# 64-row contraction tails of the w1, V, K and Q products run as row-tile pairs, and PSUM evacuated two banks at a time, in a fused attention and MLP block

## The chip, the cores and the metric

The kernel runs on one core of one Trainium2 chip. The metric is the device time of one execution in microseconds (us). Each execution also has a *span*, the time from its first to its last instruction; here the time is 1.7 to 2.9 us more than the span. Stage times below are read on the span's clock. Every run lists the clock granted to TensorE.

The engines are PE (TensorE; PEld is its weight load), ACT (ScalarE), DVE (VectorE), POOL (GpSimd) and SP (which here only issues DMAs).

## The reference

```
xn = layernorm(x)                       # x: 2048 x 448, bf16
# A: linear attention, 16 heads of 28
q, k, v = xn @ wqkv
phi(t)  = [softmax(t @ w_phi), softmax(-(t @ w_phi))]      # per head
A       = (phi(q) @ (phi(k)^T v)) / (phi(q) . sum phi(k) + 1e-6) @ wo
# B: MLP with token shifts
h   = gelu(layernorm(xn) @ w1)          # four column quarters, shifted by +1, -1, +2, -2 tokens
x1  = xn + shifted(h) @ w2
B   = x1 + gelu(layernorm(x1) @ w3) @ w4                   # w3: 448 x 1792
out = x + A + B
```

What matters for this change is the 448. It is contracted in every product with xn, and 448 = 3 x 128 + 64: three full passes of 128 rows through the PE array and a *tail* of 64 rows.

## The kernel before

One program covers three stages, which overlap at their edges:

1. **Head.** The layer norm of 16 token tiles (statistics on DVE; scales on POOL; the multiply-add `ln_apply` of even tiles on POOL and odd ones on DVE from tile 4 on). The normalized tiles are transposed into `xnT`: tiles 0 to 11 by PE, tiles 12 to 15 by DMA. V of tiles 0 to 7 and the w1 product follow. w_phi is folded into the q and k weights (`fold`).
2. **K/Q stage.** K, Q, the later V tiles, w2, and the accumulation `kv_tile`.
3. **Tail stage.** The w3 product, with w4, the numerators of the attention and the output woven in.

A recorder gathers all operations in program order, each goes to its engine's queue, and semaphores are worked out from the tiles that are read and written. So each engine runs its own operations strictly in the order of the program text. All matmuls are recorded by one helper line (L186 before, L188 after); one goes by tile names instead of lines.

```python
# loads: rows 64..127 of the fourth row block are zero (a memset), so that a tail is a full 128-row matmul
def load_rows(dst, src):
    R.dma(dst[:, 0:3, :], src[0:384, :].rearrange("(c p) d -> p c d", p=128))
    R.dma(dst[0:64, 3, :], src[384:448, :])
# ... (cut)
R.ew(dve, "memset", xn[:, :, D:512], 0.0)           # columns 448..511 of xn
R.ew(dve, "memset", wv[64:128, 3, :], 0.0)
R.ew(dve, "memset", w1[64:128, 3, :], 0.0)
# ... (cut)
def ln_apply(eng, dst, src, rst, i):
    R.ew(eng, "tensor_scalar", dst, src, rst[:, i, 1:2], rst[:, i, 0:1], op0=ALU.add, op1=ALU.mult)

def ln1_apply(a, n, engs):
    for i in range(a, a + n):
        ln_apply(engs[i % len(engs)], xn[:, i, 0:D], xtok[:, i, :], rs, i)

def w1_chunk(g, m):                                 # 4 slots: three full passes and the zero-padded tail
    b = bank(2, 3, 4)
    for kc in range(KC):
        R.mm(b[0:CR, :], w1[:, kc, CR*m:CR*m+CR], xnT[:, kc, 512*g:512*g+512], kc == 0, kc == KC - 1)
    R.act(hT[0:CR, m, 2+512*g:2+512*g+512], b[0:CR, :], ACT.Gelu_apprx_tanh)

def k_tile(i):                                      # v_tile and q_chunk have the same form
    b = rot_b()                                     # a ring of six banks in this stage
    for kc in range(KC):
        R.mm(b[:, 0:D], xnT[:, kc, 128*i:128*i+128], wpk[:, kc, :], kc == 0, kc == KC - 1)
    R.act(phik[:, i, 0, :], b[:, 0:D], ACT.Exp)
    R.act(phik[:, i, 1, :], b[:, 0:D], ACT.Exp, scale=-1.0)
    # ... (cut: sums on DVE, the softmax's multiply on POOL)

def w3_quad(q):                                     # already uses row-tile pairs
    gf = [divmod(4 * q + k, FC) for k in range(4)]
    for k, (g, fc) in enumerate(gf):
        for kc in range(3):
            R.mm(banks[k][:, :], w3[:, kc, 128*fc:128*fc+128], gT[:, g % 2, kc, :], kc == 0, False)
    for k, (g, fc) in enumerate(gf):
        lo = 64 * (k % 2)
        R.mm(banks[k][:, :], w3[lo:lo+64, 3, 128*fc:128*fc+128], gT[lo:lo+64, g % 2, 3, :], False, True)
    for k, (g, fc) in enumerate(gf):
        R.act(h3T[:, g % 2, fc, :], banks[k][:, :], ACT.Gelu_apprx_tanh)
# ... (cut)
for g in (2, 3):                                    # end of the head
    for m in range(NM):
        fold(3 - g, m)
        w1_chunk(g, m)
for i in range(NT):                                 # the K/Q stage: a fine weave of single banks
    k_tile(i)
    if i >= 2:
        kv_tile(i - 2)
    if i % 2 == 0:
        v_tile(8 + i // 2)
    else:
        w2_tile(i // 2)
    q_chunk(*divmod(i, 4))
    # ... (cut: ln_scale, g_apply, g_T)
```

`w3_quad` shows the idea that the change extends. It puts four outputs in four banks and does their full passes first. Then come the four 64-row tails, alternately on rows 0 to 63 and rows 64 to 127. The tail rows of both operands lie on both halves, so that two tails run at once.

The softmax here doesn't subtract the row's maximum and nothing guards it: scores larger than these inputs give would overflow.

## Time and profile before

| | before |
|---|---|
| time | 200.66 us, median of 3 runs (200.6 to 200.78) |
| span of the profiled run | 198.6 us |
| head (to the first K matmul) | 34.6 us |
| K/Q stage (to the first w3 quad) | 44.4 us |
| tail stage | 119.6 us |

The first view is the page of the kernel before: busy time of each engine with its share of the span, then the shares of the chain of work that ended last.

```profile
PE 185.4 (93%) x1103; PEld 98.3 (49%) x1113; DVE 109.4 (55%) x249; ACT 87.2 (44%) x167; POOL 102.9 (52%) x155
...
PE 67%; POOL 12%; DVE 11%; DMA 3%; ACT 2%; issue 2%; SPq 1%; DVEq 0%; POOLq 0%
```

PE is busy for 93% of the span and carries most of the chain. Only a PE slot removed, or a PE wait removed, can shorten the kernel.

The next view is PE's timeline of the kernel before, in pieces. Columns are: start in us, duration, engine, line, operation, output<-inputs, shapes, count and, in brackets, idle time before the group and what ended it. Groups overlap a little, since a matmul is pipelined into the next. So one takes the distance from start to start, the *cadence*, for what a group costs.

```profile
30.55 1.03 PE L186 MATMUL bank<-xnT,w 128*112 128x512 bf16 x4
...
34.61 0.92 PE L186 MATMUL bank<-wpk,xnT 128*128 128x448 bf16 x4
...
51.34 0.92 PE L186 MATMUL bank<-wpk,xnT 128*128 128x448 bf16 x4
52.10 0.55 PE L186 MATMUL bank<-phik,vaug 128*128 128x224 bf16 x4
...
53.24 1.03 PE L186 MATMUL bank<-xnT,wpq 128*112 128x512 bf16 x4
54.10 0.92 PE L186 MATMUL bank<-wpk,xnT 128*128 128x448 bf16 x4
...
83.34 3.29 PE L186 MATMUL bank<-gT,w 128*128 128x512 bf16 x16
86.57 0.56 PE L186 MATMUL bank<-phik,vaug 128*128 128x224 bf16 x4
```

Four 448-column slots take 52.10 - 51.34 = 0.76 us (0.19 each), four 512-column slots 54.10 - 53.24 = 0.86 us (0.2155 each), a kv tile 0.38 us. No brackets: from 41.04 us on, this stage runs without a gap. (Before that PE waits once, 0.76 us at 41.04, for a kv tile's input `phik` from POOL; not shown.) The Trainium skill, "TensorE: Matmul & The Clock Gate", Part 1, gives the warm start-to-start time as N / 2.4 GHz plus about 2.5 ns, 215.7 ns at 512 columns; this trace agrees.

The w3 quad has 12 full slots and 4 tails, which as pairs count for 2. That is 14 x 0.2155 = 3.02 us, but it takes 86.57 - 83.34 = 3.23. The weight loads of the kernel before show where the other 0.2 us lies:

```profile
86.02 0.11 PEld L186 LDWEIGHTS bank<-gT,w 64*128 64x128 bf16 x4 [0.42 <-issue]
86.56 0.31 PEld L186 LDWEIGHTS bank<-phik,vaug 128*128 128x128 bf16 x4 [0.42 <-issue]
```

Twice, weight loading pauses for 0.42 us: before the first 64-row load, and before the first full-row load after the tails. The next weights aren't loaded ahead across a change of mode. The Trainium skill, "TensorEngine Tiling (Array Packing)", Key Properties, says that changing the tiling mode drains TensorE; the trace agrees, and puts the price at about 0.1 us per change.

The last view of before is POOL's timeline in the head, where the layer norm is made. One period makes two tiles.

```profile
14.79 0.70 POOL L198 TENSOR_TENSOR rs<-rs,mhalf 128x2 f32<-128x2 f32 x1
15.59 0.82 POOL L198 TENSOR_SCALAR xn<-xtok,rs 128x448 bf16<-128x448 bf16 x1
...
17.05 0.70 POOL L198 TENSOR_TENSOR rs<-rs,mhalf 128x2 f32<-128x2 f32 x1
```

The period is 17.05 - 14.79 = 2.26 us, and no line has an idle time in brackets. POOL is the engine that limits when normalized tiles appear.

### The profile page before, as it was taken

To read this page: it belongs to the slowest core of one execution; us is meant where nothing else is said; L and a number is where in the kernel's file an instruction comes from. 1 tells how busy PE (TensorE), PEld (TensorE's weight loads), DVE (VectorE), ACT (ScalarE), POOL (GpSimd) and SP (SyncE) were. 2 spreads that over 40 slices of the span, in tenths; PEclk is the share of its full clock that TensorE was granted. 3 is DMA by queue.
4 is the path that set the end of the run, shared out by engine and by line. 5 is a ranking of instruction groups with operands and counts; after the bars stand their busy time and mean duration, and the time that the engine had idled before them with its cause. 6 is when DMAs were issued, how large, how long until landed. Compare 5 with 4: busy or idle time off the path is not lost.

```text
span 198.6 us, 2932 instructions
## 1 busy us (share of the span) xinstructions
PE 185.4 (93%) x1103; PEld 98.3 (49%) x1113; DVE 109.4 (55%) x249; ACT 87.2 (44%) x167; POOL 102.9 (52%) x155
## 2 busy tenths in 40 slices
PE   0699999989999999999989999999998999999984
PEld 0345566546566665454445454454454445545541
DVE  5497410388888888557853654534255355165531
ACT  2368899966677666844404304124120430440000
POOL 7568880075668996860439333144733330313370
PEclk9999999999999999999999999999999999999999
DMA  5994259950000121032023133010416202212211
GB/s 161 284 242 92 40 93 327 289 165 0 0 0 3 26 53 26 0 56 53 10 43 78 28 76 76 3 50 14 90 26 102 53 23 50 53 25 74 50 50 48
DMA packets 32619, 14.56 MB, mean 73 GB/s; under 512 B 24414, under 2 KB 32094, under 8 KB 32606
## 3 DMA queue, kind: packets, MB, share of 16 engines
q1 hardware_dynamic: 32606, 14.39, 30.3%
q8 instruction: 8, 0.13, 0.3%
q14 instruction: 5, 0.04, 0.1%
HBM read 6.91 MB, written 1.84 MB: 44 GB/s over the span
## 4 chain that ended last, share of the span: by engine, by line
PE 67%; POOL 12%; DVE 11%; DMA 3%; ACT 2%; issue 2%; SPq 1%; DVEq 0%; POOLq 0%
PE bank L186 66%; DVE vaug L198 8%; POOL vaug L198 4%; POOL xnT L198 3%; POOL g_tok L198 2%; DMA gT<-g_tok 2%; POOL rs L198 2%; PE bank L190 1%; DMA xnT<-xnT 1%; POOL phik L198 1%; DVE xn L198 1%; SPq L201 1%; ACT L194 1%; DVE st L198 1%; DVE ksum L198 1%
## 5 line engine op out<-in xcount | busy, mean ns | idle before, releaser
L194 ACT ACTIVATE phik<-bank 128x512 bf16<-128x512 f32 (+1 forms) x88 | 44.6, 585 | 68.1 <-PE bank L186 68.0
L198 DVE TENSOR_TENSOR vaug<-bank,vaug 128x464 f32<-128x464 f32 (+2 forms) x64 | 33.3, 520 | 45.6 <-POOL vaug L198 25.7
L186 PE MATMUL bank<-gT,w 128*128 128x512 bf16 (+1 forms) x214 | 44.7, 379 | 1.4 <-DMA gT<-g_tok 0.8
L186 PE MATMUL bank<-w,phik 128*128 128x448 bf16 x224 | 45.1, 353 | 0.5 <-DVE vaug L198 0.5
L198 POOL TENSOR_TENSOR xnT<-vaug 128x448 bf16<-128x448 f32 x16 | 15.0, 940 | 53.9 <-DVE vaug L198 53.9
L198 POOL TENSOR_TENSOR phik<-phik,rks 128x896 bf16<-128x896 bf16 x16 | 27.1, 1697 | 19.5 <-DVE rks L198 19.4
L186 PEld LDWEIGHTS bank<-w,phik 128*128 128x128 bf16 x224 | 21.2, 98 | 21.6 <-issue 1.7
L186 PEld LDWEIGHTS bank<-gT,w 128*128 128x128 bf16 (+1 forms) x224 | 17.4, 97 | 23.8 <-issue 7.2
L198 DVE TENSOR_REDUCE ksum<-phik 128x32 f32<-128x896 bf16 x16 | 17.3, 1083 | 18.1 <-ACT phik L194 18.1
L198 POOL TENSOR_SCALAR g_tok<-xn,rs 128x448 bf16<-128x448 bf16 (+1 forms) x32 | 17.2, 556 | 0.0
L186 PE MATMUL bank<-xnT,wpq 128*112 128x512 bf16 x64 | 16.4, 379 | 0.0
L198 POOL TENSOR_TENSOR vaug<-xn,xtok 128x448 f32<-128x448 bf16 x16 | 16.4, 1032 | 0.0
L186 PE MATMUL bank<-wv,xnT 128*128 128x448 bf16 x64 | 15.7, 378 | 0.5 <-ACT xnT L194 0.4
L186 PE MATMUL bank<-xnT,w 128*112 128x512 bf16 x64 | 16.2, 380 | 0.0
L186 PE MATMUL bank<-wo,xnT 128*128 128x448 bf16 x64 | 14.7, 352 | 0.5 <-DMA xnT<-xnT 0.5
L186 PE MATMUL bank<-wpk,xnT 128*128 128x448 bf16 x64 | 14.7, 352 | 0.0
L186 PE MATMUL bank<-w,hT 112*128 112x448 bf16 x64 | 14.6, 354 | 0.0
L198 DVE TENSOR_TENSOR xn<-bank,xn 128x448 bf16<-128x448 f32 x16 | 9.4, 589 | 7.6 <-PE bank L186 7.6
L198 POOL TENSOR_SCALAR rs<-mv 128x2 f32<-128x2 f32 (+2 forms) x26 | 5.1, 195 | 13.9 <-DVE mv L198 12.1
L194 ACT ACTIVATE hi<-bank 112x512 bf16<-112x512 f32 x16 | 8.7, 594 | 6.5 <-PE bank L186 6.5
L194 ACT ACTIVATE eq_lo<-bank 112x512 bf16<-112x512 f32 x16 | 8.7, 595 | 5.8 <-PE bank L186 5.8
L190 PE MATMUL bank<-ident,xn 128*128 128x128 bf16 x48 | 4.9, 234 | 6.7 <-DVE xn L198 6.6
(62 smaller groups left out, 190.8 us busy)
## 6 DMA issues: line engine op xcount, KB each, us to landing
out_dram<-vaug SPq DMA_DIRECT2D x16, 112.0 KB, 1.9
w<-in_B_w_dram SPq DMA_DIRECT2D x1, 1568.0 KB, 11.5
xtok<-in_A_x_dram SPq DMA_DIRECT2D x3, 448.0 KB, 5.9
w<-in_B_w_dram SPq DMA_DIRECT2D x1, 1344.0 KB, 6.2
w<-in_B_w_dram SPq DMA_DIRECT2D x2, 224.0 KB, 6.7
w<-in_B_w_dram SPq DMA_DIRECT2D x1, 392.0 KB, 7.8
wv<-in_A_wqkv_dram SPq DMA_DIRECT2D x1, 336.0 KB, 3.8
w<-in_B_w_dram SPq DMA_DIRECT2D x1, 336.0 KB, 4.2
```

Source lines behind the costliest of these rows:

```text
L186: self.op("PE", lambda e: e.matmul(out, lhsT, rhs, start=start, stop=stop, skip_group_check=True), [out], [lhsT, rhs])
L190: self.op("PE", lambda e: e.transpose(out, in_, ident), [out], [in_, ident])
L194: self.op("ACT", lambda e: e.activation(out, in_, func, **kw), [out], [in_] + aps)
L198: self.op(eng, lambda e: getattr(e, name)(out, *args, **kw), [out], aps)
L201: self.op(eng, lambda e: e.dma_start_transpose(out, in_), [out], [in_], dma=True)
```

## The change

**Intent.** (a) Do for w1, V, K and Q what `w3_quad` does: 16 new quads in which 16 slots become 14. (b) Let one ScalarE or VectorE instruction evacuate two neighbouring PSUM banks, to save fixed cost per instruction.

For the pairs, the tail rows must lie on both partition halves. The weights of V and w1 are loaded twice; the folded q and k weights are doubled by two POOL copies (not in the cut diff). In `xnT` the doubling happens before the transpose: the layer norm writes columns 384 to 447 of each tile a second time into columns 448 to 511.

```diff
+        pairs = []                        # four PSUM tensors of two banks
+        banks = [pairs[b // 2][:, 512 * (b % 2):512 * (b % 2) + 512] for b in range(8)]
...
+        def load_dup(dst, src, eng):
+            R.dma(dst[0:64, 3, :], src[384:448, :], eng)
+            R.dma(dst[64:128, 3, :], src[384:448, :], eng)
-        R.ew(dve, "memset", xn[:, :, D:512], 0.0)
-        R.ew(dve, "memset", wv[64:128, 3, :], 0.0)
-        R.ew(dve, "memset", w1[64:128, 3, :], 0.0)
...
                 ln_apply(engs[i % len(engs)], xn[:, i, 0:D], xtok[:, i, :], rs, i)
+                ln_apply(engs[i % len(engs)], xn[:, i, D:512], xtok[:, i, 384:D], rs, i)
...
+        def quad(bs, outs, lhs, rhs, fills=()):
+            for k in range(4):
+                for kc in range(3):
+                    R.mm(outs(banks[bs[k]]), lhs(k, kc, 0, 128), rhs(k, kc, 0, 128), kc == 0, False)
+                # (cut: transposes and folds put in between)
+            for k in range(4):
+                lo = 64 * (k % 2)
+                R.mm(outs(banks[bs[k]]), lhs(k, 3, lo, lo + 64), rhs(k, 3, lo, lo + 64), False, True)
+        # w1_quad, v_quad, kq_quad (two K tiles and two Q chunks) use it; in kq_quad:
+            for s in range(2):            # one Exp for two K tiles, then one for two Q chunks
+                R.act(phik[:, i:i + 2, s, :], two(bs[0])[:, :, 0:D], ACT.Exp, scale=1.0 - 2.0 * s)
+            for s in range(2):
+                R.act(e[:, :, s, :], two(bs[2])[0:CR, :, :], ACT.Exp, scale=1.0 - 2.0 * s)
...
+        w2s = {0: 0, 2: 2, 4: 4, 5: 6, 6: 8, 7: 10}     # K/Q stage in 8 steps on a ring of 3 bank pairs
+        for ps in range(8):
+            kq_quad(2 * ps, take(4))
+            # two w2 tiles, or (steps 1 and 3) a v_quad, then two kv tiles
...
-            [(W, 8), (kv_tile, 14), (ga, 1)],           # the tail stage's plan, first lines
-            [(kv_tile, 15), (kv_copy,), (W, 9), (W, 10), (kv_blocks,), (G, 4), (G, 5)],
+            [(kv_tile, 13), (kv_tile, 14), (W, 12), (ga, 1)],
+            [(kv_tile, 15), (kv_copy,), (W, 13), (W, 14), (kv_blocks,), (G, 4), (G, 5)],
```

(The diff is cut and shortened.) Four w2 tiles move from the tail stage into the K/Q stage, and one kv tile moves the other way.

## The prediction

> **What bounds it now.** The table of busy time has TensorE (PE) at 93% of 198.6 us (VectorE 55%); the chain of waits is 67% PE, nearly unbroken from 25 to 79 us. The timeline gives cadences: a 512-column matmul every 0.2155 us, a 448-column one 0.19, a kv tile 0.38. So only removed PE slots or stalls move the time. Stages: head to 34.6 us, K/Q stage to 79.0, tail.
>
> **Removed.** 16 quads turn 16 slots into 12 full plus 4 tails that should take 2: nominally 4 x 0.43 (w1) + 4 x 0.38 (V) + 8 x 0.405 (K/Q) = 6.5 us. But the w3 quads already do this, and the timeline shows one taking 3.23 us, not 14 x 0.2155 = 3.02: the 64-row weight loads start only when the last full matmul is through (0.42 us "issue" wait), and the next full-row load waits again: 0.1 us per switch. The Trainium skill, "TensorEngine Tiling (Array Packing)", Key Properties: a change of tiling mode drains TensorE; this trace agrees. Net: 3.3 us. ScalarE saves about 0.06 us per merged instruction (estimate: two K exps take 0.98 us at 0.553 us duration), but is 68% busy in 41-79 us: worth nothing directly.
>
> **Added.** The layer norm's second 128x64 write per tile: 0.395 us on POOL (same form in g_tok), about 0.13 us (estimate) on DVE. From 12 to 25 us POOL runs the norm back to back, 2.26 us per two tiles; that becomes about 2.65. Tile 14 comes 2.5 us later (25.5 to 28 us). Before, the DMA transposes of tiles 12-15 (issued 23.2-28.65) were in time for w1 group 3 at 30.55; now the last lands at about 32.5. PE also waits 0.5-1 us at the transposes of tiles 3, 6, 8 and 10, asked for earlier now. Head: 34.6 becomes 36.5 us.
>
> **K/Q stage.** PE: minus 2.0 (tails), plus 3.0 (four w2 tiles brought forward), minus 0.4 (one kv tile moved back). New stalls: at the start the next quad waits for the table load and four two-bank exps (0.8-0.9 us each): 0.9 us; 0.3 us where a V quad follows on the same ring, twice; POOL (two norms of 1.7, g_tok 2.2, rs 1.5 in one 5.3 us step) delays a kv tile 0.7 us. The old 0.76 us stall goes. Stage 44.4 becomes about 46.3.
>
> **Tail.** Loses four w2 tiles (3.0), gains a kv tile (0.4); part of the 0.85 us wait for gT near 153 us may go; ga(1) on POOL ends later and may cost as much. About -3.
>
> Sum: +2 +2 -3, less a share for overstated stalls: **200.4 us** (0.1% faster). 8 in 10: **197.0 to 203.2**. Faster by over 2%: 0.17; within 2%: 0.75; slower: 0.08.
>
> **What would show it.** Each quad takes 0.2 us over its 14 slots. POOL's period per two tiles in the head is 2.6-2.8 us; PE idles at transposes (released by POOL xn) and before w1 group 3 (released by DMA xnT); the first K matmul is at 36-37 us. First w3 matmul at 82-83.5 us; then 116.5 us to the end.
>
> **What would make it wrong.** If the small POOL write is hidden or costs under 0.2 us, or the transposes' landing isn't awaited, the head gains: 197 us. If 448-column tails switch without waits, another 3 us off. If two-bank exps cost more than twice one bank's cadence, or the bank ring stalls each K/Q step: 203 or more.

## The result, and the profile after

| | before | after |
|---|---|---|
| time, same rounds | 200.63 us (200.26 to 200.78, 4 runs) | 202.44 us (202.19 to 203.5, 4 runs) |
| ratio | | 1.0103, 95% interval 1.0064 to 1.0142 |
| span of the profiled run | 198.6 | 200.6 |
| head | 34.6 | 36.9 (+2.3) |
| K/Q stage | 44.4 | 47.6 (+3.2) |
| tail stage | 119.6 | 116.2 (-3.4) |

A ratio here is the mean time of one kernel's runs over that of the other's of the same rounds, so it isn't quite the ratio of the medians that are quoted. The changed kernel is about 1% slower: within 2%, and inside the predicted range. The stage differences sum to the span's +2.0 us. Of the stage changes, +3.0 and -3.0 us are only the four moved w2 tiles, and -0.4 and +0.4 us the moved kv tile (the durations are PE slots: 4 x 0.76, and 0.38). So moved work makes up 2.7 us of the K/Q stage's +3.2 and of the tail stage's -3.4.

The page of the kernel after:

```profile
PE 185.0 (92%) x1113; PEld 91.3 (46%) x1113; DVE 111.0 (55%) x251; ACT 81.0 (40%) x95; POOL 105.6 (53%) x163
...
PE 57%; POOL 18%; DVE 10%; ACT 5%; DMA 5%; issue 3%; SPq 0%; DVEq 0%; POOLq 0%
```

PE's busy time hardly moved, though slots worth 6.5 us nominally were removed. It is a poor measure here. The Trainium skill, "Perfetto Trace Analysis", Tensor Engine Instruction, says that the end of a matmul is estimated by the profiler and not observed. This trace agrees: a 512-column matmul has a mean duration of about 0.38 us while the next starts after 0.2155, so a drain or a wait of up to 0.17 us behind it counts as busy. The chain says more: PE's share fell from 67 to 57%, POOL's rose from 12 to 18%, DMA's and ACT's rose too.

POOL's timeline of the kernel after, in the head:

```profile
15.97 0.70 POOL L200 TENSOR_TENSOR rs<-rs,mhalf 128x2 f32<-128x2 f32 x1
16.77 1.21 POOL L200 TENSOR_SCALAR xn<-xtok,rs 128x448 bf16<-128x448 bf16 x2
...
18.62 0.70 POOL L200 TENSOR_TENSOR rs<-rs,mhalf 128x2 f32<-128x2 f32 x1
```

The period per two tiles is now 18.62 - 15.97 = 2.65 us, against 2.26: the small second write adds 0.39 us per POOL tile, almost half of the 448-column write (0.82), for a seventh of its columns. The norm of the last tiles comes that much later, and so do the DMA transposes of tiles 12 to 15. The chain of the kernel after (start, duration, what) shows them on the critical path:

```profile
29.99 2.49 DMA xnT<-xn
...
32.61 0.83 PE bank L188 x3
```

The last transpose lands at 29.99 + 2.49 = 32.48, and the fourth w1 group begins at 32.61. Before, it began at 30.55, with all transposes landed. PE's timeline of the kernel after, in pieces:

```profile
17.66 0.83 PE L192 MATMUL bank<-ident,xn 128*128 128x128 bf16 x8 [0.52 <-POOL xn L200]
...
22.98 0.61 PE L192 MATMUL bank<-ident,xn 128*128 128x128 bf16 x4 [0.69 <-POOL xn L200]
...
39.92 1.69 PE L188 MATMUL bank<-w,hT 112*128 112x448 bf16 x8
41.87 1.31 PE L188 MATMUL bank<-wpk,xnT 128*128 128x448 bf16 x6 [0.26 <-ACT phik L196]
43.70 1.50 PE L188 MATMUL bank<-xnT,wpq 128*112 128x512 bf16 x6 [0.52 <-ACT eq_lo L196]
...
47.32 1.79 PE L188 MATMUL bank<-wv,xnT 128*128 128x448 bf16 x10 [0.37 <-ACT phik L196]
49.04 0.56 PE L188 MATMUL bank<-phik,vaug 128*128 128x224 bf16 x4
...
62.10 1.30 PE L188 MATMUL bank<-wpk,xnT 128*128 128x448 bf16 x6
...
67.43 1.30 PE L188 MATMUL bank<-wpk,xnT 128*128 128x448 bf16 x6
68.63 1.50 PE L188 MATMUL bank<-xnT,wpq 128*112 128x512 bf16 x6
...
72.87 0.92 PE L188 MATMUL bank<-wpk,xnT 128*128 128x448 bf16 x4
...
83.00 0.93 PE L188 MATMUL bank<-phik,vaug 128*128 128x224 bf16 x8
84.43 3.29 PE L188 MATMUL bank<-gT,w 128*128 128x512 bf16 x16 [0.51 <-DMA gT<-g_tok]
```

Three things are to be read here.

- In the head, PE waits for POOL's normalized tiles (0.52 and 0.69 us), and for DVE's at tiles 2 and 3 (0.93 us in two waits, not shown).
- In the K/Q stage there are waits "<-ACT": a quad asks for a bank whose exps are not done. The listed idle times understate them for the reason just given. Eight w2 slots from 39.92 end at 39.92 + 8 x 0.19 = 41.44, so the wait to 41.87 is 0.43 us and not 0.26. In the same way 0.52 is 0.69 and 0.51 is 0.67. Two more, inside the two V quads (0.37 listed at 47.32, and 0.36), are 0.54 and 0.53. In four more steps, without brackets, the cadence is 72.87 - 67.43 = 5.44 us where 67.43 - 62.10 = 5.33 is possible: 0.11 each. The sum, with the wait of the next point, is 3.3 us.
- The first w3 quad waits 0.67 us for gT's DMA, since its input g_tok came late from POOL.

The K/Q stage thus adds up: moved work +2.7, tails saved -2.0 (8 quads at 0.2, 2 at 0.18), waits +3.3, the old wait for `phik` -0.9 (0.76 listed); together about +3.1 us, where +3.2 was measured.

The tail stage gained a little by itself, about 0.8 us beyond the moved work: before, PE had idled 0.85 us for gT's DMA at 153 us; after, there is no such gap.

### The profile page after: what moved, and what is told of

Same layout as the page of the kernel before. It is cut to its first block, busy times and chain, and to the rows that moved or that the text cites. A ratio compares the mean times of both kernels' runs of the same rounds, so it can differ in the third digit from the quotient of the medians.

```text
span 200.6 us, 2895 instructions
## 1 busy us (share of the span) xinstructions
PE 185.0 (92%) x1113; PEld 91.3 (46%) x1113; DVE 111.0 (55%) x251; ACT 81.0 (40%) x95; POOL 105.6 (53%) x163
## 4 chain that ended last, share of the span: by engine, by line
PE 57%; POOL 18%; DVE 10%; ACT 5%; DMA 5%; issue 3%; SPq 0%; DVEq 0%; POOLq 0%
PE bank L188 57%; POOL rs L200 6%; DVE vaug L200 6%; POOL xn L200 3%; POOL phik L200 3%; ACT phik L196 3%; POOL g_tok L200 2%; DVE st L200 2%; POOL xnT L200 2%; POOL vaug L200 2%; DVE xn L200 1%; DMA gT<-g_tok 1%; DMA xnT<-xn 1%; DMA xnT<-xnT 1%; DMA xtok<-in_A_x_dram 1%
## 5 line engine op out<-in xcount | busy, mean ns | idle before, releaser
L196 ACT ACTIVATE phik<-bank 128x1024 bf16<-128x1024 f32 (+1 forms) x44 | 40.9, 982 | 83.4 <-PE bank L188 83.4
L188 PE MATMUL bank<-gT,w 128*128 128x512 bf16 (+1 forms) x224 | 46.2, 379 | 0.5 <-DMA gT<-g_tok 0.5
L188 PE MATMUL bank<-xnT,wpq 128*112 128x512 bf16 (+1 forms) x64 | 14.9, 382 | 0.5 <-ACT eq_lo L196 0.5
L188 PE MATMUL bank<-xnT,w 128*112 128x512 bf16 (+1 forms) x64 | 15.3, 387 | 0.1
L188 PE MATMUL bank<-wv,xnT 128*128 128x448 bf16 (+1 forms) x64 | 13.7, 374 | 1.1 <-ACT phik L196 0.7
L192 PE MATMUL bank<-ident,xn 128*128 128x128 bf16 x48 | 5.5, 235 | 9.0 <-DVE xn L200 7.6
L188 PE MATMUL bank<-w,hT 112*128 112x448 bf16 x64 | 13.7, 354 | 0.0
L188 PE MATMUL bank<-wpk,xnT 128*128 128x448 bf16 (+1 forms) x64 | 13.3, 355 | 0.3 <-ACT phik L196 0.3
L200 DVE TENSOR_SCALAR xn<-xtok,rs 128x448 bf16<-128x448 bf16 (+1 forms) x18 | 7.8, 474 | 5.7 <-POOL rs L200 5.7
L200 DVE BATCH_NORM_STATS2 st<-xtok 128x6 f32<-128x448 bf16 x16 | 9.7, 604 | 1.9 <-DMA xtok<-in_A_x_dram 1.9
```

The lines of the kernel that those rows point to most:

```text
L188: self.op("PE", lambda e: e.matmul(out, lhsT, rhs, start=start, stop=stop, skip_group_check=True), [out], [lhsT, rhs])
L192: self.op("PE", lambda e: e.transpose(out, in_, ident), [out], [in_, ident])
L196: self.op("ACT", lambda e: e.activation(out, in_, func, **kw), [out], [in_] + aps)
L200: self.op(eng, lambda e: getattr(e, name)(out, *args, **kw), [out], aps)
```

## The experiments

Theory 1, mine after the result: the second write of the layer norm costs the head about 2 us, evacuation by bank pairs stalls the K/Q stage, and the paired tails give less than nominal because of the mode changes. The rivals: the pairs themselves are at fault (drains eat them whole); or the reorder of the K/Q stage is; or the saved ScalarE time is worth something and only the doubling hurts. Twelve runs were made, of eleven kernels, in four batches; all results were correct. In these batches the kernel before had medians of 200.46, 200.58, 200.64 and 200.47 us.

| kernel | median us (runs) | ratio to before | first K | first w3 quad | span |
|---|---|---|---|---|---|
| before | 200.6 | 1 | 34.6 | 79.0 | 198.6 |
| after | 202.44 (4) | 1.0103 | 36.9 | 84.4 | 200.6 |
| b_dup | 204.36 (5) | 1.0181 | 39.0 | 83.3 | 202.7 |
| a_full_dup | 203.07 (4) | 1.0129 | 37.2 | 85.4 | 201.3 |
| a_full_nodup | 202.8 (6) | 1.0088 | 35.1 | 83.3 | 199.3 |
| a_dup_tr5 | 202.01 (5) | 1.0076 | 36.5 | 84.3 | 200.3 |
| a_dup_act | 204.88 (6) | 1.0202 | 39.5 | 87.1 | 203.1 |
| a_one_bank | 200.86 (6) | 1.0016 | 36.6 | 82.9 | 199.0 |
| a_w3_split | 204.88 (4) | 1.0219 | 36.8 | 84.3 | 203.0 |
| best_v1 | 201.85 (6) | 1.0062 | 41.1 (V quad at 38.3) | 85.3 | 200.1 |
| best_v2 | 206.98 (6) | 1.0314 | 42.6 | 87.4 | 203.7 |
| best_v3 | 197.73 (5) | 0.9865 | 35.2 | 80.0 | 196.3 |
| best_v4 | 198.99 (5) | 0.9930 | 34.8 | 81.0 | 197.3 |

"First K", "first w3 quad" and "span" are of the profiled run, in us. In some traces the first matmul record of the w3 quad is missing (15 records where 16 belong, or a first piece that is one short); the start is then set 0.22 us earlier than the first record.

### b_dup: before, with the second write alone

```diff
-        R.ew(dve, "memset", xn[:, :, D:512], 0.0)
...
                 ln_apply(engs[i % len(engs)], xn[:, i, 0:D], xtok[:, i, :], rs, i)
+                ln_apply(engs[i % len(engs)], xn[:, i, D:512], xtok[:, i, 384:D], rs, i)
```

The weights' rows 64 to 127 of the fourth block stay zero, so the result is unchanged.

> The kernel before plus only the layer norm's second 128x64 write per tile (the columns it fills meet zero weights, so the result stays right); no quads, no merged evacuation. Theory (the write loads POOL, which paces the norm, and with it the transposes of the last four tiles): POOL's period per two tiles goes from 2.26 to about 2.66 us, the last four DMA transposes are issued 26.0-31.3 instead of 23.2-28.65, w1's last group starts 1.5 us later than 30.55, and the whole takes 1.3 to 2.3 us more than before: 202.0 to 203.0. Rival (the write hides, and the change's loss sits in the K/Q stage or the tail): within 0.4 us of before.

Measured: 204.36 us (203.59 to 204.67), ratio 1.0181 (1.0156 to 1.0207). The runs fall into two groups: spans of 201.0 to 201.1 us at clock 1.0, and 202.6 to 202.7 us at clock 0.992. The profile is one of the latter. PE's timeline of b_dup:

```profile
25.55 1.03 PE L186 MATMUL bank<-xnT,w 128*112 128x512 bf16 x4
28.75 0.37 PE L186 MATMUL bank<-bd,hi 112*128 112x112 bf16 x4 [2.18 <-DVE bd L198]
...
30.02 1.90 PE L186 MATMUL bank<-xnT,w 128*112 128x512 bf16 x4
```

DVE makes `bd` only after its part of the norm, which waits for POOL's scales; PE idles 2.18 us for it. A little later the same four matmuls take 1.90 us in place of 1.03. The windows view of b_dup (columns: stretch, length, busy time of each engine with counts, granted clock, DMA share, GB/s) shows why:

```profile
30.00:33.70 3.70, 3.70 (x18) 2.05 (x16) 0.00 (x0) 2.06 (x4) 2.08 (x10) 0.54 0.55 120
```

The granted clock was 0.54 for 3.7 us, which costs about 1.6 us. What follows: the second write alone costs 2.4 us of span in the runs without the clock loss and 4.0 with it (3.2 and about 4 us of device time). I had expected 1.3 to 2.3 us, by way of the late DMA transposes; the loss came by another way, the wait for `bd`. In the kernel after, that wait is just 0.17 us, since its order is another, and the clock stays up. So b_dup shows that the write delays the norm, and PE with it; it doesn't measure the loss in the head of the kernel after.

### a_full_dup and a_full_nodup: after, with full 128-row tails, with and without the second write

```diff
-                lo = 64 * (k % 2)
-                R.mm(outs(banks[bs[k]]), lhs(k, 3, lo, lo + 64), rhs(k, 3, lo, lo + 64), False, True)
+                R.mm(outs(banks[bs[k]]), lhs(k, 3, 0, 128), rhs(k, 3, 0, 128), False, True)
```

The weights' second tail rows are zero again; `a_full_nodup` also drops the second `ln_apply` and sets the columns to zero once.

> The changed kernel with every tail of the w1, V, K and Q quads as a full-row matmul against zeroed rows: 16 slots per quad, no change of tiling mode in them; all else of the change stays. Theory (a pair of switches costs 0.2 us, so a quad gains only about 0.2 us): 1.8 to 3.3 us slower than the changed kernel, 204.2 to 205.8, the first K matmul 0.5-1.3 us later and the K/Q stage 1.2-2.0 us longer. Rival (pairs pay in full, two slots per quad): about 6 us slower, 208 or more.

> The same full-row tails, and the second write of the norm taken out too. The difference from the kernel with full tails and the write is the write's price in the changed order. Theory: 1.5 to 2.5 us faster than that one (POOL period back at 2.26 us, first K matmul near 35.5), so 202.2 to 203.8. Rival (the write hides): the same time as that one within 0.4 us.

Measured: a_full_dup 203.07 us (203.04 to 203.22), ratio 1.0129 (1.0104 to 1.0154). a_full_nodup 202.8 us (201.0 to 203.23), ratio 1.0088 (1.0051 to 1.0125), in two groups: spans of 199.3 us (two runs, one of them profiled) and 200.9 to 201.2 us (four runs), all at clock 1.0.

The pairs in all 16 quads are thus worth only about 0.7 us of span (201.3 - 200.6), not 6.5, and not the 1.8 to 3.3 that I expected. PE's timeline of a_full_dup shows a K/Q step in full:

```profile
62.80 1.30 PE L188 MATMUL bank<-wpk,xnT 128*128 128x448 bf16 x6
...
68.33 0.92 PE L188 MATMUL bank<-wpk,xnT 128*128 128x448 bf16 x4
```

A step with full tails takes 5.53 us and is bound by PE. With pairs, PE would need 5.33, but most steps without listed idle time take 5.44: half the gain goes to waits for banks. In the head the first K matmul moved by 0.35 us alone, since the head waits for the norm.

The second write: with it the first K matmul is at 37.2 us, without it at 35.1. That is 2.1 us between the two profiled runs. The medians differ by 0.3 us only, because four of six runs of a_full_nodup were in the longer group. What those runs wait for was not seen (see a_full_nodup_again). So my expectation of 1.5 to 2.5 us is met by the profiled pair and not by the medians.

### a_dup_tr5: the doubling by PE in place of POOL

For tiles 0 to 11 the second write is dropped, and a fifth transpose of 64 columns puts the tail into the upper half:

```diff
-                R.tr(tview(b)[:, 128*kc:128*kc+128], xn[:, i, 128*kc:128*kc+128], ident[:, :])
+                c0 = 128 * kc if kc < 3 else D - 128
+                R.tr(tview(b)[:, 128*kc:128*kc+128], xn[:, i, c0:c0+128], ident[:, :])
+            R.tr(tview(b)[0:64, 384:512], xn[:, i, 384:D], ident[:, :])
```

(The fourth full transpose takes columns 320 to 447, so that its upper half is the tail; the fifth overwrites the lower half.) The write stays for tiles 12 to 15, which DMA transposes.

> The changed kernel with the doubled tail columns made by a fifth, 64-column PE transpose for tiles 0 to 11 instead of by the norm's second write (tiles 12 to 15, which are transposed by DMA, keep the write). Pairs stay. Theory: POOL's period is back at 2.26 us for tiles 4 to 10, 12 more PE transposes cost about 0.1 us each, the first K matmul comes 0.8-1.7 us earlier than 36.87, and the whole takes 200.6 to 201.7 us. Rival (the write hides): 12 more transposes make it 0.5-1.2 us slower than the changed kernel.

Measured: 202.01 us (201.73 to 202.26), ratio 1.0076 (1.0056 to 1.0095). A miss: I had expected 200.6 to 201.7, and 0.1 us per extra transpose. PE's timeline of a_dup_tr5:

```profile
15.09 0.56 PE L192 MATMUL bank<-ident,xn 128*128 128x128 bf16 x5
15.58 0.85 PE L188 MATMUL bank<-xnT,w 128*112 128x512 bf16 x3
```

POOL's period went back to 2.26 us and PE's listed waits for xn after tile 1 are gone. But a tile's transposes now take 15.58 - 15.09 = 0.49 us, against 0.22 for four in the kernel after (15.23 to 15.45). The weight load of the fifth is listed with a tile of 128*64, in the first tiles after a pause of 0.20 us. So it may be a change of mode there and back (an estimate: two changes of 0.1 us and a slot of 0.06); no run tested that. 12 x 0.27 = 3.2 us of PE time ate what the norm gave back; the first K matmul came 0.4 us earlier. So POOL's share was a cause of the head's loss, and its removal helped only as much as the new PE work allowed.

### a_dup_act: the doubling by ScalarE

```diff
+        def dup(i):
+            R.act(xn[:, i, D:512], xn[:, i, 384:D], ACT.Copy)
...
         def xn_T(i, b):
             b = banks[b]
+            dup(i)
```

> The changed kernel with the doubled tail columns written by ScalarE: a 128x64 copy of the finished columns of xn, one per tile, in place of the norm's second write on POOL and VectorE. Pairs and all else stay, and PE gets no extra work. Theory (the second write's cost is that it sits on POOL and VectorE, which pace the norm): POOL's period per two tiles is back at 2.26 us, the first K matmul comes at 34.2-35.3 instead of 36.87, the whole takes 200.0 to 201.2 us. Rival (any copy ahead of the transposes costs as much by its latency): within 0.5 us of 202.4.

Measured: 204.88 us (203.84 to 205.25), ratio 1.0202 (1.0176 to 1.0228), span 203.1. This was a miss: I had expected a gain. ScalarE's timeline of a_dup_act:

```profile
20.84 1.93 ACT L196 ACTIVATE hT<-bank 112x1024 bf16<-112x1024 f32 x2
22.64 0.27 ACT L196 ACTIVATE xn<-xn 128x64 bf16<-128x64 bf16 x1
```

and PE's:

```profile
22.97 0.23 PE L192 MATMUL bank<-ident,xn 128*128 128x128 bf16 x1 [0.64 <-ACT xn L196]
```

The copy is cheap (0.27 us), and POOL's period was 2.26 again. But ScalarE runs in order: the copy of a tile sits behind two 0.9 us gelus, and PE waits for it. There were four such waits of 0.36 to 0.67 us. Not all of the loss is theirs: in this profile the first V quad took 3.24 us (11.99 to 15.23), and in best_v1, which has the same head, 2.01 us. Why isn't known; the granted clock reads 1.00 in both. Without this best_v1's head ended at 38.3 us, still 1.4 later than that of the kernel after. The runs of a_dup_act form two groups (spans of 202.1 and of 203.0 to 203.4 us), which this would fit. The cheapest engine by duration is not the cheapest by position in its queue.

### a_one_bank: after, with one PSUM bank per evacuating instruction

```diff
-                R.act(phik[:, i:i + 2, s, :], two(bs[0])[:, :, 0:D], ACT.Exp, scale=1.0 - 2.0 * s)
+            for j in range(2):
+                for s in range(2):
+                    R.act(phik[:, i + j, s, :], banks[bs[j]][:, 0:D], ACT.Exp, scale=1.0 - 2.0 * s)
```

and likewise for Q, w1, V and w3.

> The changed kernel with one PSUM bank per evacuating instruction again (K bank 0 both signs, then bank 1, then the Q banks; gelus, V copies and w3's gelus bank by bank). Quads and the norm's write stay. Theory (ScalarE is not the bound; what counts is when the next quad's banks come free, and a merged instruction holds both banks to its end): ScalarE works about 0.26 us more per K/Q step, but the first banks come free earlier, the waits of the first two K/Q steps shrink by 0.3-0.8 us, and the steps with w2 take 5.33 instead of 5.45 us: 0.3 to 1.5 us faster than the changed kernel. Rival (the merged instruction is what lets ScalarE keep up): 0.5 us or more slower.

Measured: 200.86 us (200.69 to 201.24), ratio 1.0016 (0.9999 to 1.0034), span 199.0. The merged evacuation costs the changed kernel about 1.6 us; undoing it alone brings it level with before. ScalarE in the kernel after (first fence) and in a_one_bank (second), for the same kind of step:

```profile
65.03 1.73 ACT L196 ACTIVATE phik<-bank 128x896 bf16<-128x896 f32 x2 [3.66 <-PE bank L188]
66.64 1.94 ACT L196 ACTIVATE hi<-bank 112x1024 bf16<-112x1024 f32 x2
```

```profile
63.46 1.85 ACT L196 ACTIVATE phik<-bank 128x448 bf16<-128x448 f32 x4 [2.97 <-PE bank L188]
65.17 2.08 ACT L196 ACTIVATE hi<-bank 112x512 bf16<-112x512 f32 x4
```

PE's timeline of a_one_bank:

```profile
45.09 3.02 PE L188 MATMUL bank<-wv,xnT 128*128 128x448 bf16 x16
48.04 0.56 PE L188 MATMUL bank<-phik,vaug 128*128 128x224 bf16 x4
...
60.54 1.30 PE L188 MATMUL bank<-wpk,xnT 128*128 128x448 bf16 x6
...
65.87 1.30 PE L188 MATMUL bank<-wpk,xnT 128*128 128x448 bf16 x6
67.00 1.46 PE L188 MATMUL bank<-xnT,wpq 128*112 128x512 bf16 x6
```

Merged, ScalarE works from 65.03 to 68.58, or 3.55 us; with single banks from 63.46 to 67.25, 3.79 us. Merging saves 0.24 us of ScalarE. Yet the next Q matmuls, which need the Q pair's banks, start at 68.63 in the kernel after, just after the last merged exp ends at 68.58. In a_one_bank they start at 67.00, 0.25 us *before* ScalarE is through, because the first of the two banks was free by then. The steps are 5.33 us exactly (65.87 - 60.54). That is 0.11 us in each of four steps. More comes from the V quads: one takes 48.04 - 45.09 = 2.95 us here, 0.09 over its slots and mode changes, where the kernel after waits 0.54 us at 47.32. By stage, the head is 0.26 us shorter than in the kernel after, the K/Q stage 1.25 and the tail stage 0.1. In the K/Q stage the waits fell from 3.3 to 2.1 us: 1.12 to 0.87 in the second step, 1.07 to 0.18 in the two V quads, 0.44 to nothing in the steps with w2; the wait for POOL's part before the first w3 quad grew from 0.67 to 1.07. ScalarE wasn't the limit; how soon a bank is free was. The Trainium skill, "TensorEngine Tiling (Array Packing)", PSUM Bottleneck, warns that tiling speeds up TensorE but not the evacuation. This trace agrees: a quad makes four banks ready within a few tenths of a microsecond, and their evacuation takes 3.5 us.

### a_w3_split: twice the mode changes in the w3 quads

```diff
+            for h in (0, 2):              # full passes of two, their pair of tails, then the other two
-            for k, (g, fc) in enumerate(gf):
+                for k, (g, fc) in list(enumerate(gf))[h:h + 2]:
```

The work is the same; each w3 quad changes mode four times rather than twice.

> The changed kernel with each w3 quad (in the tail, where PE alone is the bound) running its pairs in two halves: six full matmuls, one pair, six full, one pair. Same matmuls, twice as many changes of tiling mode. Theory (0.1 us per change): each w3 quad takes 3.43 instead of 3.23 us, 14 of them 2.8 us; tail from 116.2 to 119 us, total 204.6 to 205.7. Rival (the missing 0.2 us per quad is slower streaming of 64-row matmuls, not the change of mode): the same time within 0.4 us.

Measured: 204.88 us (204.85 to 205.33), ratio 1.0219 (1.0199 to 1.0239), span 203.0. PE's timeline of a_w3_split:

```profile
89.25 3.51 PE L188 MATMUL bank<-gT,w 128*128 128x512 bf16 x16
92.69 0.56 PE L188 MATMUL bank<-phik,vaug 128*128 128x224 bf16 x4
```

The quad takes 92.69 - 89.25 = 3.44 us against 3.23: two more changes cost 0.21 us. For 14 quads that is 2.9 us; the span grew by 2.4 (203.0 - 200.6), and the tail stage took 118.7 us against 116.2. So the drain of about 0.1 us per change is a real cost and nearly all of it is on the critical path. It doesn't eat the pairs whole: a quad with pairs is still 0.2 us shorter than one with full tails (5.33 against 5.53 us per step).

### best_v1: ScalarE doubling and a reordered K/Q stage

```diff
+        v_quad(8, (4, 5, 6, 7))           # moved ahead of the first K/Q quad
         for ps in range(8):
-            kq_quad(2 * ps, take(4))
+            kq_quad(2 * ps, (0, 1, 2, 3))  # K/Q always on the same four banks
```

(with `a_dup_act`'s copies and two more w2 tiles in the stage.)

> The ScalarE copies, and the K/Q stage in another order: V tiles 8-11 before the first K/Q quad (so that ScalarE can load its table meanwhile), K/Q quads always on banks 0-3, the other V quad on banks 4-7 before kv needs them, fourteen w2 tiles in this stage, the first g_apply one step earlier. Theory: the waits for ScalarE in the first steps (0.26+0.52+0.37+0.36 us) and the 0.51 us wait for gT go, and with the head's gain the whole takes 197.8 to 199.8 us, faster than both kernels. Rival (the stage is bound by VectorE and POOL, whose work per step is 5.5 us): no faster than the kernel with the ScalarE copies alone.

Measured: 201.85 us (201.6 to 202.0), ratio 1.0062 (1.0046 to 1.0077). A miss too: I had expected under 200. The new order did take most of the stage's waits away: by the cadence 0.16 and 0.68 us (0.51 listed) are left in the second step and 0.11 in each of four steps, 1.3 us in all against 3.3. But the head kept a_dup_act's fault. Since the head is the same, a_dup_act is the control for the stage: its runs have spans of 202.1 and 203.0 to 203.4 us, best_v1's 199.9 to 200.3. So the reordered stage (with two more w2 tiles and an earlier `g_apply`) is worth about 2 us, with the merged evacuation kept. What the merge costs thus depends on the order in which the banks come round.

### best_v2: before's head, doubling by DMA, after's K/Q stage

The layer norm writes nothing twice; the tail rows are copied from SBUF to SBUF after the transposes. The head is before's, the K/Q stage is after's with one bank per evacuation, and `g_apply` comes a step earlier so that gT is in time for the first w3 quad.

```diff
+        for g in range(4):                # issued right after the DMA transposes, ahead of load_rest
+            R.dma(xnT[64:128, 3, 512*g:512*g+512], xnT[0:64, 3, 512*g:512*g+512])
```

> What the runs so far point to: the head of the kernel before (no quads, no second write in the norm, zeroed rows), the doubled rows made by four SBUF-to-SBUF DMAs after the transposes, the changed kernel's K/Q stage with its pairs but one bank per evacuating instruction, g_apply of the first four tiles one step earlier. Theory: first K matmul at 34.4-34.9, K/Q stage about 46 us as with one-bank evacuation, no wait for gT before the first w3 quad, tail 116.2: span 196.4 to 197.4, time 198.2 to 199.3 us, about 1% faster than before. Rival (the early stage sets VectorE and POOL back, so what PE saves returns as waits at the first w3 quads): 200 us or more.

Measured: 206.98 us (205.45 to 207.66), ratio 1.0314 (1.028 to 1.0348), clock 0.983. My own mistake: the head's zero-padded w1 products also read the rows 64 to 127 (times zero), and in program order the copies came before w1 groups 2 and 3. So those groups waited for them: PE idled 5.93 us, and the next matmuls ran at a low clock. A read that is multiplied by zero is still a read that waits.

### a_full_nodup_again: one more look at the split runs

> The same kernel as a_full_nodup, whose six runs fell in two groups (span 199.3 twice, 200.9-201.2 four times) at full clock. One more look, for a profile of the longer group if it falls there. If the head is what varies, the first K matmul comes near 36.8 instead of 35.09; if the tail is, the first w3 matmul stays at 83.5.

Measured: 201.16 us in one run, span 199.3, state unknown. The run fell in the shorter group again. What the longer group waits for stays open. (One lead, not tested: a slow first V quad, as in the profile of a_dup_act, would pass to the end in a head that hardly waits for the norm.)

### best_v3 and best_v4: best_v2 mended, and the same without pairs

```diff
-        for g in range(4):
+        for g in range(2):                # groups whose w1 products are already recorded
             R.dma(xnT[64:128, 3, 512*g:512*g+512], xnT[0:64, 3, 512*g:512*g+512])
...
+        for g in range(2, 4):             # after the w1 products, before the K/Q stage; w4's load after it
+            R.dma(xnT[64:128, 3, 512*g:512*g+512], xnT[0:64, 3, 512*g:512*g+512])
```

In best_v4 the K/Q and V quads of this kernel have full 128-row tails again and nothing is doubled; all else is the same.

> best_v2 with its own mistake mended: the doubling DMAs of groups 2 and 3, for which w1's last two groups waited 5.9 us, now come after those groups, and w4's load after them. Head of before, pairs in the K/Q and V quads of the K/Q stage only, one bank per evacuation, g_apply one step earlier. Theory: first K matmul at 34.4-34.9, first w3 matmul at 80.2-81.0, tail 116.2: span 196.3 to 197.3, time 198.1 to 199.2 us, about 1% faster than before. Rival (the K/Q stage's VectorE and POOL work, 5.5 us per step, is the floor): 199.5 us or more.

> best_v3 without any pair of row tiles in w1, V, K and Q: full-row tails against zeroed rows, no doubling DMAs. The difference from best_v3 is what the pairs are worth where nothing else is paid for them (8 K/Q quads at 0.2 us, 2 V quads at 0.18). Theory: 1.5 to 2.1 us slower than best_v3, with each K/Q step with w2 at 5.53 instead of 5.33 us; time 199.8 to 201.2. Rival (VectorE and POOL set the step): the same as best_v3 within 0.4 us.

Measured: best_v3 197.73 us (196.99 to 198.35), ratio 0.9865 (0.9841 to 0.989). best_v4 198.99 us (198.89 to 199.18), ratio 0.9930 (0.9917 to 0.9944). Best_v3 beats both kernels, by 1.35% against before; that is under the 2% that count as faster, but clear of noise. It did better than expected (198.1 to 199.2), and so did best_v4 (199.8 to 201.2). PE's timeline of best_v3:

```profile
58.70 1.30 PE L188 MATMUL bank<-wpk,xnT 128*128 128x448 bf16 x6
...
64.03 1.30 PE L188 MATMUL bank<-wpk,xnT 128*128 128x448 bf16 x6
...
80.24 3.08 PE L188 MATMUL bank<-gT,w 128*128 128x512 bf16 x15
```

The step is 5.33 us, and no wait for gT stands before the w3 quad (15 of its 16 records are there). The head ends at 35.2 us as against 36.9 in the kernel after. Sixteen quads of pairs brought 0.7 us beside the second write and the merged evacuation. The ten of the K/Q stage bring 1.26 us here (198.99 - 197.73), where neither gets in their way; I had expected 1.5 to 2.1. Of best_v3's total gain on before of 2.7 us, about 1.5 us (200.47 - 198.99) comes from what best_v4 changes, in the main the new order of the K/Q stage with gT in time, and not from the pairs. Both long waits of the kernel before, 0.76 us for `phik` and 0.85 us for gT, are absent from best_v4's list of waits; the two were not tried one by one. So the order of the K/Q stage is not at fault either, once its banks come free one by one.

## Why the prediction was right or wrong

The outcome, "within 2%" at 200.4 us with 197.0 to 203.2, held: 202.44 us. But the range was wide, and the centre was 2 us off, and the terms say why.

- **What bounds the kernel: right.** PE at 93%, and each change was worth what it did to PE's waits and slots.
- **"Net: 3.3 us" for the pairs: right in each quad, wrong at the end.** Quads took 0.2 us over their 14 slots, as the w3 quads had shown (a_w3_split shows that cost by doubling it). But only 0.7 us reached the end (a_full_dup), since the head waits for the norm and the K/Q steps for banks.
- **The second write on POOL: right.** A period of 2.65 us was predicted and measured. "The last lands at about 32.5": 32.48. First K matmul "at 36-37": 36.87. The head grew by 2.26 us where I had 1.9. The runs in pairs (b_dup against before, a_full_dup against a_full_nodup in the profiled group) give 2.4 and 2.1 us of span, the first by another way (the wait for `bd`).
- **The second write on DVE: mis-sized.** I estimated 0.13 us. DVE's timeline of the kernel after has a pair of writes, the large and the small, from 16.70 for 0.93 us, ending at 17.63. With POOL idle the pair takes 0.61 us (at 6.78), the small write 0.29 of it; beside POOL's writes the small one was put down as 0.55 on the mean. In the pair from 16.70, POOL's 448-column write runs from 16.77 to 17.59. The Trainium skill, "SBUF — State Buffer", "Summary: rules for kernel authors", says that with DVE in its two-port mode beside GpSimd the second to issue blocks until the first is done. The trace fits that (DVE's pair ends 0.04 us after POOL's write), but no run tested it. The cost isn't small: before POOL sets the pace, the norm goes through DVE. Its longer pairs (0.21 us at 6.78, 0.53 at 10.25) delay POOL's scales for tiles 4 and 5 by 0.77 us (12.74 against 11.97 in the kernel before). Five periods of 0.39 on POOL then make it 2.77 us at tile 14 (27.41 against 24.64). So over a quarter of the norm's delay is DVE's.
- **"ScalarE saves ... worth nothing directly": right, but this was the failing step's other side.** The term for the K/Q stage was "New stalls" of 0.9 + 0.3 twice + 0.7, that is 2.2 us; measured were 3.3. The kinds of wait were right, the sizes weren't: 1.12 us in the second step for 0.9, 0.54 and 0.53 in the V quads for 0.3 each, 0.67 for POOL's 0.7, and 0.44 in the steps with w2, where none was predicted. I had counted a longer instruction there and not that *both* its banks stay shut until it ends. The stage ended at 84.4 us, not at 82 to 83.5. My own list under "What would make it wrong" has it: "the bank ring stalls each K/Q step: 203 or more". A_one_bank shows it: 1.6 us back by undoing only the merge, most of it in this stage.
- **"POOL ... delays a kv tile 0.7 us": wrong place.** No kv tile waited. POOL's lag came out instead as 0.67 us before the first w3 quad, through g_tok and gT's DMA, so the size was right by luck.
- **The tail stage: right.** 116.5 us predicted, 116.2 measured; of the 0.85 us wait for gT at 153 us, all went.
- **"Less a share for overstated stalls": the failing step.** The terms as predicted, +2 +2 -3 (measured: +2.3 +3.2 -3.4), made a span of 199.6, which with the usual 1.9 us is 201.5 us. I then took 1.1 us off, on the feeling that PE stalls tend to be overstated. They were understated: by the profile itself (0.17 us per wait, because matmul ends are modelled) and by my sum (1.1 us). Without the deduction the prediction would have been within 1 us.

In sum, the change pays in the right currency, PE slots, but pays for it where the slots can't be collected. The doubled write delays the norm, on which the head waits. The quad brings four banks to their end at once, and the merged instruction then returns them in twos. The merge is shown by undoing it alone (1.6 us in the medians). That the second write delays the head is shown by adding it alone (2.4 us of span at full clock, though by the wait for `bd`) and, in the profiled runs, by dropping it (2.1 us). Its price in the kernel after is less certain: dropped from the kernel with full tails it gave back only 0.3 us in the medians, for a reason that stays open. The pairs bring 0.7 us to the end here, of 3.3 net in PE slots (1.26 of 2.0 in best_v3), which doesn't pay for the two.

Two things stay open: the two groups of runs of a_full_nodup (the longer was never profiled), and whether best_v1's order of banks would add to single-bank evacuation, since no run has both.

## What to carry to other kernels

An instruction that evacuates two PSUM banks frees none until it has finished both; where PE waits for banks, the shorter total loses to the earlier release, so merge only where the bank ring has slack. Price a data layout that a PE trick needs (here doubled rows) on the engine and at the place in its queue where it must be made: POOL in the norm, ScalarE behind gelus and PE as a fifth transpose all lost, and copies by DMA that PE did not have to wait for won. When the terms of a prediction are each read from a trace, leave their sum alone: here a deduction without a source made it worse.

## What the Trainium skill lacked or had wrong

- "TensorEngine Tiling (Array Packing)", Key Properties, says that a change of mode drains TensorE but gives no size. Here it was about 0.1 us per change: 3.23 us for a quad of 14 slots (3.02 us) with two changes, and 3.44 us with four.
- The same page, Theoretical Speedup, promises up to 2x for 64-row contractions. For a tail of 64 rows behind three full passes, a quad saved 0.2 us of about 3.2 us (16 slots to 14, less the two changes), and 0.7 us (16 quads) or 1.26 us (10 quads) of 200 in the whole kernel, depending on what else waits.
- The same page, PSUM Bottleneck, advises vectorizing PSUM access across tiles of one bank. It says nothing of one instruction over two banks, where both stay shut until it ends. Here that saved 0.24 us of ScalarE per step and cost 1.6 us in all, on a ring of three pairs of banks.
- "TensorE: Matmul & The Clock Gate", Part 1, has the clock fall after at least one idle window of about 3.4 us. Here an idle time of 2.18 us was followed, about 1.3 us after its end, by 3.7 us at a granted clock of 0.54. That was in one group of b_dup's runs (mean clock 0.992); in the other the mean clock was 1.0. The page calls the window free-running, which would fit two groups; no run here shows it.
- No page prices a transpose whose stationary operand has 64 columns among others of 128: the fifth one added 0.27 us to a tile's 0.22 us of four. Its weight load is listed with a tile of 128*64, so this may be the first point again, two changes of mode; no run tested it.
- "GPSIMD Engine Reference", in its table that reconciles the measured numbers, names the dispatch hops of a GpSimd instruction and gives no time for them (its section on instruction dispatch has only "tens of cycles" for one of them). Here a 128x64 write on GpSimd took 0.39 us and a 128x448 one 0.82 us. A straight line through the two gives 1.1 ns per column and a fixed part of 0.32 us (an estimate from these two numbers; 0.34 from the same writes of g_tok, 0.40 and 0.72 us), which is why a seventh of the columns costs almost half the time.
